# Channel attention, then a GELU feed-forward in split precision: Strassen's seven products in the second layer too, in chunks of 512 tokens

## The chip, the cores and the metric

The kernel runs on 1 core of a Trainium2 chip. The metric is device time in microseconds; before the change it is 2187.15 us (median of three runs, 2186.88 to 2187.25). TensorE does the matmuls, VectorE (DVE) and ScalarE (ACT) the elementwise work, GpSimd (POOL) next to nothing, SyncE (SP) issues the transfers. SBUF is the on-chip memory of 128 partitions, PSUM the accumulators of the matmuls: 8 banks, each 128 partitions by 512 fp32 values.

## The reference

```python
# attention: B, N, C = 4, 6080, 256
qn = q / (norm(q, axis=1, keepdims=True) + 1e-06)        # k likewise
s = kn.transpose(0, 2, 1) @ qn / tau                     # 256 x 256 for each of 4 batches
a = softmax(s, axis=-1)
x = (v @ a).reshape(24320, 256)
# feed-forward: w_in 256 x 2048, w_out 2048 x 256
h = x @ w_in
g = 0.5 * h * (1.0 + erf(h / sqrt(2)))
out = g @ w_out
```

The weights reach the kernel as fp64 words and are narrowed on the chip.

## The kernel before, in words

**Numbers.** Each fp32 operand is split into a high part in fp32r, the matmul format, and a low part with the rest. A product is three matmuls: low weight by high data, high by high, high weight by low data. Making a pair costs an ACT write of the high part and a DVE subtraction for the low part.

**Stages.** For each batch, the scores of q and k give `a`; `w_group` (L365) folds `a` into `w_in`, so that the feed-forward's first layer takes v directly. Batch 0's scores come first, alone. Those of batch b+1 are made in small pieces during the feed-forward of batch b: `extras` (L653) puts pieces behind each step: `load_qk`, `split_qk` (L178), `burst` (L186, which adds its PSUM bank to `sacc` at L201), `norm_part` (L203), the softmax, and the next `w_group`s.

**Feed-forward.** A batch's 6080 tokens are cut into 6 pairs of token blocks (five of 2 x 512 tokens, one of 2 x 480), and the 2048 hidden features into 8 units u of 256. One step is (batch, pair, unit).

- First layer (`first_products`, L484): the step's block of h, 2 feature rows by 2 token columns, by Strassen's seven products in Winograd's form, with the v forms (B11, T1, ...) and weight forms (A11, S1, ...) prepared ahead by `v_sums`, `v_split` and `w_sums`. Seven products of three 512-column matmuls (L458 to L460). Three partial sums are copied to SBUF by ACT (`kept`, L491), three joins are DVE additions of a PSUM bank and such a copy (`added`, L496). Then `gelu` (L462) twice on ACT, to high format (L466) and to fp32 (L467), and a DVE subtraction for the low part (L468).
- Second layer (`second_products`, L528): the plain way, 2 token blocks x 2 feature rows x 2 output halves, three matmuls each (L541 to L543), 24 matmuls a step, summed over the eight units in four PSUM banks `po`. After the last unit ACT and DVE move them to `osb`, and they go out.
- The first pair of batch 0 uses plain products in both layers (`plain_products`, L471), while `narrow_unit` (L576) still narrows weights.

**Order.** The program is written so that each yield of the first layer's product is followed by one part of the *previous* step's second layer (L714, L715): on TensorE, first-layer and second-layer matmuls alternate in threes. From this order a planner makes each engine's queue: it may take a later instruction ahead where an earlier one would not be ready by its own costs. Each queue then runs strictly in its order on the chip. `issue_after` (in `behind`, L105) holds named instructions behind a mark.

**Buffers.** PSUM: four banks `ph` for the first layer, bursts and weight groups (`bank`, L111), four for `po`. `w_out` units come back from a DRAM copy (`keep_out`, L255) through three `wo` buffers, one load of 512 KB a step (`load_wo`, L268).

## Time and profile before

| | |
|---|---|
| time of the runs | 2187.15 us (2186.88 to 2187.25) |
| profiled execution, its span | 2185.0 us (the page gives no other time of that execution) |
| TensorE matmuls, weight loads | 9664, 9664 |
| TensorE / DVE / ACT busy | 2174.5 / 1392.8 / 1437.0 us |
| matmul groups of the two layers, L458-460 and L541-543 | 1564.0 us and 1800.0 us, with overlap |
| DMA | 267.52 MB, mean 122 GB/s |

The page sums an instruction from its start to its modelled end. Neighbours on one engine overlap, so the spacing of starts in a timeline, not the mean of one instruction, is what a long queue costs. Where a line has several shapes, the answers that keep shapes apart are used.

### The profile page before, as it was taken

How to read it: one execution, taken by the hardware profiler on the slowest of the kernel's cores; microseconds unless marked ns; L12 is line 12 of the kernel's file. 1: busy time of each engine (PE TensorE's matmuls, PEld its weight loads, DVE VectorE, ACT ScalarE, POOL GpSimd, SP SyncE). 2: the span in 40 equal slices, each digit the busy share in tenths (PEclk: the TensorE clock that was granted, in tenths of full speed). 3: DMA queues.
4: the chain of work that ended last, by engine and by line, in shares of the span. 5: the costliest groups of instructions: out<-in, count | busy, mean ns of one | idle time of the engine just before them, and what ended most of it. 6: DMA issues, size and time to landing. Idle time of an engine off the chain costs nothing.

```text
span 2185.0 us, 26209 instructions
## 1 busy us (share of the span) xinstructions
PE 2174.5 (100%) x9664; PEld 1793.9 (82%) x9664; DVE 1392.8 (64%) x2179; ACT 1437.0 (66%) x2595; POOL 1.3 (0%) x8
## 2 busy tenths in 40 slices
PE   9999999999999999999999999999999999999999
PEld 7788888888888888888888888888888888888888
DVE  6995767656676575675667757657466555555554
ACT  6666666667666666676765666667576566666665
POOL 0000000000000000000000000000000000000000
PEclk9999999999999999999999999999999999999999
DMA  9562534422343353542323335343132122121121
GB/s 380 189 211 106 174 133 157 160 90 87 106 144 105 118 173 116 174 154 67 105 92 134 122 116 174 133 153 128 49 112 97 58 89 71 65 97 66 68 78 47
DMA packets 77056, 267.52 MB, mean 122 GB/s; under 512 B 7680, under 2 KB 9728, under 8 KB 74880
## 3 DMA queue, kind: packets, MB, share of 16 engines
q1 hardware_dynamic: 76928, 265.84, 35.2%
q8 instruction: 76, 1.25, 0.2%
q14 instruction: 52, 0.43, 0.1%
HBM read 232.52 MB, written 33.29 MB: 122 GB/s over the span
## 4 chain that ended last, share of the span: by engine, by line
PE 97%; DVE 2%; DMA 1%; issue 0%; ACT 0%; SPq 0%; DVEq 0%; ACTq 0%
PE po L543 16%; PE po L541 16%; PE po L542 16%; PE ph L460 14%; PE ph L459 14%; PE ph L458 14%; PE ph L191 3%; PE ph L193 1%; DMA raw<-qk 1%; DVE acc L139 1%; PE ph L378 1%; PE ph L376 1%; PE ph L377 1%; PE ph L149 0%; DVE nt L247 0%
## 5 line engine op out<-in xcount | busy, mean ns | idle before, releaser
L468 DVE TENSOR_TENSOR gl<-g,gh 128x512 fp32r<-128x512 f32 (+1 forms) x768 | 521.7, 682 | 145.3 <-ACT g L467 142.7
L543 PE MATMUL po<-gl,wo 128*128 128x512 f32 (+1 forms) x1536 | 605.2, 394 | 0.0
L541 PE MATMUL po<-gh,wo 128*128 128x512 f32 (+1 forms) x1536 | 599.2, 390 | 0.6 <-ACT gh L466 0.6
L542 PE MATMUL po<-gh,wo 128*128 128x512 f32 (+1 forms) x1536 | 595.6, 388 | 0.0
L496 DVE TENSOR_TENSOR h<-ph,p 128x512 f32<-128x512 f32 (+1 forms) x368 | 252.0, 685 | 531.4 <-PE ph L460 452.6
L460 PE MATMUL ph<-vl,wh 128*128 128x512 f32 (+1 forms) x1336 | 522.7, 391 | 0.0
L459 PE MATMUL ph<-vh,wh 128*128 128x512 f32 (+1 forms) x1336 | 521.5, 390 | 0.0
L458 PE MATMUL ph<-vh,wl 128*128 128x512 f32 (+1 forms) x1336 | 519.8, 389 | 0.7 <-DVE wl L363 0.7
L466 ACT ACTIVATE gh<-h 128x512 fp32r<-128x512 f32 (+1 forms) x552 | 345.2, 625 | 236.8 <-DVE h L496 232.8
L491 ACT COPY p<-ph 128x512 f32<-128x512 f32 (+1 forms) x368 | 213.4, 583 | 241.4 <-PE ph L460 240.3
L542 PEld LDWEIGHTS po<-gh,wo 128*128 128x128 f32 x1536 | 288.4, 188 | 64.0
L541 PEld LDWEIGHTS po<-gh,wo 128*128 128x128 f32 x1536 | 288.4, 188 | 62.3 <-ACT gh L466 1.0
L543 PEld LDWEIGHTS po<-gl,wo 128*128 128x128 f32 x1536 | 288.4, 188 | 61.5
L467 ACT ACTIVATE g<-h 128x512 f32<-128x512 f32 (+1 forms) x552 | 337.5, 611 | 0.0
L459 PEld LDWEIGHTS ph<-vh,wh 128*128 128x128 f32 x1336 | 251.1, 188 | 56.9
L458 PEld LDWEIGHTS ph<-vh,wl 128*128 128x128 f32 x1336 | 251.0, 188 | 53.2 <-DVE h L496 1.4
L460 PEld LDWEIGHTS ph<-vl,wh 128*128 128x128 f32 x1336 | 250.9, 188 | 51.0
L491 ACT COPY u<-ph 128x512 f32<-128x512 f32 (+1 forms) x184 | 106.9, 581 | 106.6 <-PE ph L460 106.6
L466 ACT ACTIVATE gh<-ph 128x512 fp32r<-128x512 f32 (+1 forms) x216 | 125.3, 580 | 22.9 <-PE ph L460 18.2
L467 ACT ACTIVATE g<-ph 128x512 f32<-128x512 f32 (+1 forms) x216 | 126.5, 586 | 1.6 <-DVE gl L468 1.5
L496 DVE TENSOR_TENSOR h<-ph,u 128x512 f32<-128x512 f32 (+1 forms) x184 | 125.4, 682 | 2.8
L209 ACT ACTIVATE kqc<-kqc 128x1024 f32<-128x1024 f32 x72 | 76.4, 1061 | 36.1 <-DMA kqc<-kqt 36.0
(135 smaller groups left out, 1354.0 us busy)
## 6 DMA issues: line engine op xcount, KB each, us to landing
wo<-keep_out SPq DMA_DIRECT2D x184, 512.0 KB, 3.3
raw<-qk SPq DMA_DIRECT2D x95, 512.0 KB, 4.3
kqc<-kqt SPq DMA_DIRECT2D x72, 512.0 KB, 4.4
v_raw<-vt SPq DMA_DIRECT2D x20, 1024.0 KB, 5.5
out<-osb SPq DMA_DIRECT2D x40, 512.0 KB, 3.3
win<-keep_in SPq DMA_DIRECT2D x12, 1024.0 KB, 4.8
keep_in<-win SPq DMA_DIRECT2D x4, 1024.0 KB, 4.6
keep_out<-wo SPq DMA_DIRECT2D x8, 512.0 KB, 3.6
```

The costliest lines, as they stand in the source:

```text
L209: nc.scalar.activation(out=x, in_=x, func=AF.Square, accum_out=state["nsum"][:, t, c:c + 1])
L458: nc.tensor.matmul(ps[:, :n], wl, hi[:, :n], start=start, stop=False, skip_group_check=True)
L459: nc.tensor.matmul(ps[:, :n], wh, hi[:, :n], start=False, stop=False, skip_group_check=True)
L460: marks["product"] = nc.tensor.matmul(ps[:, :n], wh, lo[:, :n], start=False, stop=stop, skip_group_check=True)
L466: nc.scalar.activation(out=gh[:, :n], in_=src, func=AF.Gelu)
L467: marks["gelu"] = nc.scalar.activation(out=g[:, :n], in_=src, func=AF.Gelu)
L468: nc.vector.tensor_tensor(out=gl[:, :n], in0=g[:, :n], in1=f32(gh[:, :n]), op=ALU.subtract)
L491: nc.scalar.copy(out=t[:, :n], in_=ps[:, :n])
L496: nc.vector.tensor_tensor(out=h[:, :n], in0=ps[:, :n], in1=t[:, :n], op=ALU.add)
L541: nc.tensor.matmul(o, wo[:, 1, i, cs], gh[:, :n], start=first, stop=False)
L542: nc.tensor.matmul(o, wo[:, 0, i, cs], gh[:, :n], start=False, stop=False)
L543: nc.tensor.matmul(o, wo[:, 0, i, cs], gl[:, :n], start=False, stop=last)
```

## The change

**Chunks.** After the first pair the unit of work is a chunk of 512 tokens (480 at a batch's end), cut in two halves of 256 (240), by a group g of 512 features: 46 chunks x 4 groups. `chunk_products` does the first layer's seven products with two output rows q each, so 42 matmuls of 256 columns. The v forms of a chunk have double buffers.

**First layer's joins.** ACT copies product 1 into another PSUM bank `px`, and product 4 accumulates on it; DVE writes product 3's sum plus product 2's copy into a bank `pz`, and product 6 accumulates on that. Copies go from 3 to 2, additions from 3 to 2.

**Second layer.** `sums` makes four combinations (T1 to T4) of the GELU blocks, splits them, and `chunk_out` takes seven products of 2 x 3 matmuls of 256 columns with weight forms A and S (`CROSS`), summed over the groups in four banks and joined at the chunk's end on ACT and DVE. The block B12 then needs only its fp32 GELU. The last chunk of batches 0 to 2 (`plain_out`) keeps plain second-layer products of 480 columns.

**Weights of the second layer.** `wo_sums` makes the S forms once, with 24 additions on POOL, in the first pair; eight forms are kept in DRAM, and seven (1.79 MB) are loaded for each step, in four loads with a buffer each (`load_part`), each issued when the same part of the step before has been used (`load_next`).

**Other.** PSUM: two banks `ph`, one `px`, one `pz`; bursts and weight groups of later batches take turns with the products in the two `ph` banks. The high copies of `split_qk` and of `w_sums` are on ACT. `kqc` and `osb` have one buffer. The written order still alternates, now in sixes; the join of product 7 and `sums` come after the last of the previous step's second-layer products, and the extras after them.

```diff
+CHUNKS = [(t + j * n, n // 2) for t, n in PAIRS for j in range(2)]
+NCH = len(CHUNKS)
+H = NT // 2
...
+FORMS = ("S4", "A11", "A12", "S3", "S1", "S2", "A21", "A22")
+CROSS = (("S4", "B22"), ("A11", "B11"), ("A12", "B21"), ("S3", "T3"), ("S1", "T1"), ("S2", "T2"), ("A22", "T4"))
+SLOT = {"T2": 0, "T4": 1, "T1": 2, "T3": 3, "B12": 3, "B11": 4, "B22": 5, "B21": 6}
+GSLOT = {"B11": 0, "B12": 1, "B22": 2, "B21": 3}
+BLOCK = {(1, 0): "B22", (0, 1): "B11", (1, 1): "B21", (0, 0): "B12"}
...
-    ps_h = ctx.enter_context(tc.tile_pool(name="ps_h", bufs=4, space=bass.MemoryType.PSUM))
+    ps_h = ctx.enter_context(tc.tile_pool(name="ps_h", bufs=2, space=bass.MemoryType.PSUM))
+    ps_x = ctx.enter_context(tc.tile_pool(name="ps_x", bufs=1, space=bass.MemoryType.PSUM))
...
+        state["bank"] = at = (state.get("bank", -1) + 1) % 4
+        if at % 2 and "halves" not in state:
+            return ps_x.tile([P, NT], F32, name="px" if at == 1 else "pz")
         return ps_h.tile([P, NT], F32, name="ph")
...
-        nc.vector.tensor_copy(out=hl[:, 0], in_=raw)
+        nc.scalar.copy(out=hl[:, 0], in_=raw)
...
+    def load_part(b, c, g, i):
+        at, to = parts(b, c)[i]
+        t = pw.tile([P, 2, 2, 2, P], F32R, name="wo", bufs=4)
+        marks["wo"] = nc.sync.dma_start(out=f32(t[:, 0:to - at]), in_=keep_out[g][:, at:to])
+        for f in range(at, to):
+            wos[b, c, g, FORMS[f]] = t[:, f - at]
...
+    def wo_sums(g):
+
+        first = pqk.tile([P, 2, 4, 2, P], F32, name="hl")
+        fa, fs = first[:, 0], first[:, 1]
+        hl = pqk.tile([P, 4, 2, 2, P], F32R, name="hl")
+        tt = nc.gpsimd.tensor_tensor
+        for q in range(2):
+            wo = wos[0, 0, 2 * g + q]
...
+            tt(out=fa[:, :, q], in0=v[0], in1=v[1], op=ALU.add)
...
+        tt(out=s4, in0=a12, in1=s2, op=ALU.subtract)
+        nc.scalar.copy(out=hl[:, :, 0], in_=fs)
+        nc.vector.tensor_tensor(out=hl[:, :, 1], in0=fs, in1=f32(hl[:, :, 0]), op=ALU.subtract)
...
+        copy = nc.scalar.copy
...
+    def v_sums(b, c):
+        x, h = v_half(b, c)
         tt = nc.vector.tensor_tensor
-        if half == 0:
-            ts = vts[b, p] = [pv.tile([P, NT], F32, name=f"vs{i}") for i in range(4)]
-            tt(out=ts[0][:, :n], in0=x[0, 1], in1=x[0, 0], op=ALU.subtract)
-            tt(out=ts[2][:, :n], in0=x[1, 1], in1=x[0, 1], op=ALU.subtract)
+        t = vts[b, c] = pv.tile([P, 4, H], F32, name="vs")
+        tt(out=t[:, 0:2, :h], in0=x[:, :, 1], in1=x[:, 0], op=ALU.subtract)
+        tt(out=t[:, 2, :h], in0=x[:, 1, 1], in1=t[:, 0, :h], op=ALU.subtract)
+        tt(out=t[:, 3, :h], in0=x[:, 1, 0], in1=t[:, 2, :h], op=ALU.subtract)
...
         def do(i, ps, start, stop):
-            product(b, p, u, *ORDER[i], ps, start, stop)
-
-        one = bank()
+            a, v = ORDER[i]
+            at = VSLOT[v]
+            for q in range(2):
+                o = ps[:, q]
+                nc.tensor.matmul(o, wls[g][:, a, q], vh[:, at, :h], start=start and q == 0, stop=False,
+                                 skip_group_check=True)
+                nc.tensor.matmul(o, whs[g][:, a, q], vh[:, at, :h], start=False, stop=False,
+                                 skip_group_check=True)
+                marks["product"] = nc.tensor.matmul(o, whs[g][:, a, q], vl[:, at, :h], start=False, stop=stop,
+                                                    skip_group_check=True)
...
+        def block(at, src):
+            name = BLOCK[at]
+            whole = halves(gs[:, GSLOT[name]], h)
+            nc.scalar.activation(out=whole, in_=src, func=AF.Gelu)
+            if name == "B12" and not plain:
+                return
+            hi, lo = (halves(t[:, SLOT[name]], h) for t in (his, los))
+            nc.scalar.activation(out=hi, in_=src, func=AF.Gelu)
+            tt(out=lo, in0=whole, in1=f32(hi), op=ALU.subtract)
+
+        def sums():
+            t, hi, lo = (x.rearrange("p i (q n) -> p i q n", q=2)[:, :, :, :h] for x in (gs, his, los))
+            tt(out=t[:, 0:2], in0=t[:, 1:3], in1=t[:, 0:2], op=ALU.subtract)
+            nc.scalar.copy(out=hi[:, 2:4], in_=t[:, 0:2])
+            tt(out=t[:, 2], in0=t[:, 2], in1=t[:, 0], op=ALU.subtract)
+            tt(out=t[:, 3], in0=t[:, 3], in1=t[:, 2], op=ALU.subtract)
+            nc.scalar.copy(out=hi[:, 0:2], in_=t[:, 2:4])
+            tt(out=lo[:, 2:4], in0=t[:, 0:2], in1=f32(hi[:, 2:4]), op=ALU.subtract)
+            tt(out=lo[:, 0:2], in0=t[:, 2:4], in1=f32(hi[:, 0:2]), op=ALU.subtract)
+
+        one = halves(ps_h.tile([P, NT], F32, name="ph"), h)
         do(0, one, True, False)
-        p1 = kept(one, "p1")
-        yield
-        two = bank()
-        do(1, two, True, False)
-        p5 = kept(two, "p5")
+        x = halves(ps_x.tile([P, NT], F32, name="px"), h)
+        nc.scalar.copy(out=x, in_=one)
+        yield
+        two = halves(ps_h.tile([P, NT], F32, name="ph"), h)
+        do(1, two, True, True)
+        p5 = halves(pg.tile([P, NT], F32, name="p5", bufs=2), h)
+        nc.scalar.copy(out=p5, in_=two)
         yield
         do(2, one, False, False)
-        u2 = kept(one, "u2")
-        yield
-        three = bank()
-        do(3, three, True, True)
-        out[1, 0] = gelu(added(three, p1), n)
+        z = halves(ps_x.tile([P, NT], F32, name="pz"), h)
+        tt(out=z, in0=one, in1=p5, op=ALU.add)
+        yield
+        do(3, x, False, True)
+        block((1, 0), x)
         yield
         do(4, one, False, False)
-        out[0, 1] = gelu(added(one, p5), n)
-        yield
-        do(5, two, False, True)
-        out[1, 1] = gelu(added(two, u2), n)
+        tt(out=p5, in0=one, in1=p5, op=ALU.add)
+        block((0, 1), p5)
+        yield
+        do(5, z, False, True)
+        block((1, 1), z)
         yield
         do(6, one, False, True)
-        out[0, 0] = gelu(one[:, :n], n)
+        yield
+        block((0, 0), one)
+        if not plain:
+            sums()
 
...
+        for i, (form, v) in enumerate(CROSS):
+            if first and i % 2 == 0:
+                po["banks"].append(new_bank())
+            o = po["banks"][i // 2][:, i % 2]
+            w = wos.pop(key + (form,))
+            for q in range(2):
+                mh, ml = (halves(m[:, SLOT[v]], h)[:, q] for m in (his, los))
+                nc.tensor.matmul(o, w[:, 1, q], mh, start=first and i % 2 == 0 and q == 0, stop=False,
+                                 skip_group_check=True)
+                nc.tensor.matmul(o, w[:, 0, q], mh, start=False, stop=False, skip_group_check=True)
+                nc.tensor.matmul(o, w[:, 0, q], ml, start=False, stop=last and q == 1, skip_group_check=True)
+            if i % 2 or i == 6:
+                load_next(key, i // 2)
+            if last:
+                banks = po["banks"]
+                if i == 0:
+                    osb = new_osb()
+                    pq = state["pq"] = pg.tile([P, 4, H], F32, name="pq", bufs=1)[:, :, :h]
+                elif i == 1:
+                    nc.scalar.copy(out=pq[:, 0:2], in_=banks[0])
+                elif i == 3:
+                    tt(out=osb[:, 1], in0=banks[1][:, 0], in1=pq[:, 1], op=ALU.add)
+                    nc.scalar.copy(out=pq[:, 3], in_=banks[1][:, 1])
+                elif i == 5:
+                    nc.scalar.copy(out=pq[:, 2], in_=banks[2][:, 0])
+                    tt(out=osb[:, 2], in0=banks[2][:, 1], in1=pq[:, 1], op=ALU.add)
+                    tt(out=osb[:, 0:4:3], in0=pq[:, 2:4], in1=osb[:, 2:3].broadcast_to([P, 2, h]), op=ALU.add)
+                    tt(out=osb[:, 0], in0=osb[:, 0], in1=pq[:, 0], op=ALU.add)
+                    tt(out=osb[:, 2], in0=osb[:, 3], in1=pq[:, 2], op=ALU.add)
+                elif i == 6:
+                    tt(out=osb[:, 3], in0=banks[3][:, 0], in1=osb[:, 3], op=ALU.add)
+                    done()
+            yield
...
+    def extras(b, w):
+
+        c, g = divmod(w, NWG)
...
+            nxt = (b, c + 1) if c + 1 < NCH else (b + 1, 0)
+            if nxt[0] < B:
+                if c % 2 and g == 0:
+                    load_v(nxt[0], nxt[1] // 2)
+                if g == 1:
+                    v_sums(*nxt)
+                elif g == 2:
+                    v_split(*nxt, 0)
+                elif g == 3:
+                    v_split(*nxt, 1)
+                    v_split(*nxt, 2)
...
+    state["halves"] = True
+    many = 2
+    for b in range(B):
+        for c in range(0 if b else 2, NCH):
+            for g in range(NWG):
+                for _ in chunk_products(b, c, g):
+                    for _ in range(many):
+                        next(second, None)
+                for _ in second:
+                    pass
+                extras(b, c * NWG + g)
+                second = chunk_out(b, c, g)
+                many = 2 if plain_out(b, c) else 1
```

What is left out of the diff: renamed arguments, the first pair's products (as before), the plain second layer of a batch's last chunk, and the load order.

317 lines of the change are left out of this document (190 added, 127 removed).

## The prediction

> **What bounds the kernel now.** I read the page's shares first, then the chain of work that ended last, then what TensorE waited for.
>
> ```profile
> span 2185.0 us, 26209 instructions
> PE 2174.5 (100%) x9664; PEld 1793.9 (82%) x9664; DVE 1392.8 (64%) x2179; ACT 1437.0 (66%) x2595; POOL 1.3 (0%) x8
> PEclk9999999999999999999999999999999999999999
> PE 97%; DVE 2%; DMA 1%; issue 0%; ACT 0%; SPq 0%; DVEq 0%; ACTq 0%
> ```
> ```profile
> PE ph L149 <- DMA raw<-qk: 4.7, 3, 3.7
> PE po L319 <- DVE diag L314: 0.8, 1, 0.8
> PE ph L458 <- DVE wl L363: 0.7, 1, 0.7
> PE po L541 <- ACT gh L466: 0.6, 1, 0.6
> ```
>
> TensorE sets the end at full clock. Its waits are 6.8 us in all, while DVE and ACT have a third of the span free. So the change can gain only by TensorE time, and can lose by taking that free third. The time is therefore read from the spacing of matmul starts. Three pairs of batch 3 (each window runs from a pair's first product to the next pair's), a stretch of a burst with all engines, and two rows of a 480-column stretch:
>
> ```profile
> 1766.30:1849.20 82.90, 82.90 (x362) 67.64 (x361) 44.99 (x70) 54.10 (x98) 0.00 (x0) 1.00 0.22 77
> sum 248.60, PE 248.60 PEld 202.85 DVE 134.62 ACT 162.09 POOL 0.00; mean PE 82.87 PEld 67.62 DVE 44.87 ACT 54.03 POOL 0.00
> ```
> ```profile
> 1010.97 0.40 PE L191 MATMUL ph<-hl 128*128 128x512 f32 x1
> ...
> 1011.21 0.28 PE L193 MATMUL ph<-hl 128*128 128x256 f32 x1
> 1011.21 0.19 PEld L191 LDWEIGHTS ph<-hl 128*128 128x128 f32 x1
> ...
> 1011.32 0.39 PE L191 MATMUL ph<-hl 128*128 128x512 f32 x1
> ...
> 1011.55 0.28 PE L193 MATMUL ph<-hl 128*128 128x256 f32 x1
> ...
> 1012.25 0.28 PE L193 MATMUL ph<-hl 128*128 128x256 f32 x1
> ...
> 1012.56 0.69 DVE L201 TENSOR_TENSOR sacc<-ph,sacc 128x512 f32<-128x512 f32 x1 [0.58 <-PE ph L193]
> ...
> 1013.29 0.42 DVE L290 TENSOR_TENSOR t<-sacc 128x256 f32<-128x256 f32 x1
> ...
> 1013.75 0.39 PE L458 MATMUL ph<-vh,wl 128*128 128x512 f32 x1
> ...
> 1013.95 0.69 DVE L201 TENSOR_TENSOR sacc<-ph,sacc 128x512 f32<-128x512 f32 x1 [0.23 <-PE ph L193]
> ```
> ```profile
> 2172.01 0.38 PE L460 MATMUL ph<-vl,wh 128*128 128x480 f32 x1
> ...
> 2172.66 0.38 PE L543 MATMUL po<-gl,wo 128*128 128x480 f32 x1
> ```
>
> A pair is 8 x 45 = 360 matmuls: 82.87 / 360 = 0.230 us per 512 columns. Eight neighbours L191 + L193 take 1013.75 - 1010.97 = 2.78 us; less 0.230 for the 512, a 256-column matmul costs 0.117 us. Of 480 columns, three take 0.65 us: 0.217 each. A consumer starts 0.03 us after its matmul (1012.25 + 0.28 to 1012.56). And the planner does take later instructions ahead: L290, written behind both burst additions L201, runs between them.
>
> **Matmuls.** Removed: 23 pairs x 360. Added: 43 chunks x 4 x 84 = 14,448 of 256 (240) columns, and for the three plain chunks 504 of 240 and 288 of 480. A 512 pair becomes 672 x 0.117 = 78.6 us, 4.25 less; nineteen give -81. A 240-column matmul still has a full weight load beside it; I price it at 0.117 too, so the 480 pairs (360 x 0.217 = 78.1) become 78.6 in batch 3 and 504 x 0.117 + 96 x 0.217 = 79.8 in the others: +6. Sum **-75 us**. Bounds: 14,952 small matmuls make 15 us of each ns. At half of the 512's cost (0.115) it is -105; 0.120, the larger spacing that rounding of these rows allows, gives -30.
>
> The Trainium skill, "TensorE: Matmul & The Clock Gate", Part 3, says that a weight load overlaps running matmuls only where the row groups differ. By that each small matmul would wait for its load. The trace disagrees: the load for L191 and the 256-column L193 both start at 1011.21, and L191 follows 0.11 us later.
>
> **DVE and ACT.** Prices, from the answer that keeps shapes apart and a DVE timeline:
>
> ```profile
> L491 ACT COPY p<-ph 128x512 f32<-128x512 f32 x304 | 177.9, 587 | 219.3 <-PE ph L460 218.7
> L467 ACT ACTIVATE g<-ph 128x512 f32<-128x512 f32 x184 | 108.6, 591 | 1.6 <-DVE gl L468 1.5
> L182 DVE TENSOR_TENSOR hl<-raw,hl 128x1024 fp32r<-128x1024 f32 x68 | 82.4, 1218 | 0.7
> L396 DVE TENSOR_TENSOR hl<-hl 128x256 f32<-128x256 f32 x16 | 6.8, 422 | 9.5 <-ACT hl L379 9.5
> L403 ACT CAST wh<-hl 128x1024 fp32r<-128x1024 f32 x4 | 4.3, 1076 | 0.4 <-DVE hl L399 0.4
> ```
> ```profile
> 222.30 0.69 DVE L201 TENSOR_TENSOR sacc<-ph,sacc 128x512 f32<-128x512 f32 x1
> 222.90 1.22 DVE L182 TENSOR_TENSOR hl<-raw,hl 128x1024 fp32r<-128x1024 f32 x1
> 224.04 0.69 DVE L181 CAST hl<-raw 128x1024 fp32r<-128x1024 f32 x1
> ```
>
> In a queue a 512-wide DVE operation costs 0.60 us and a 1024-wide one 1.14. A cross step has seven of the first (two joins, three low parts, two sums) and three of the second (one sum, two low parts): 7.6 us, and 0.2 more where a sum needs the one just before. A chunk's v forms and output joins are five of 512 and eight of 256 (0.42): 6.4 us, 1.6 a step. DVE: **9.4 us a step**, against 84 x 0.117 = **9.83 on TensorE**. In batches 0 to 2 the scores and weight groups of the next batch add 1.2 to DVE (per batch 24 low parts at 1.14, 24 additions at 0.60, 4 x 3.8 of weight sums, over 48 steps) and 0.93 to TensorE (12 x 2.78 and 48 x 0.23): 10.6 against 10.76. DVE goes from 64% to about 97% of TensorE. ACT, at full durations: two copies, five GELUs from PSUM, two of B11 (priced alike), two 1024 copies, 7.5 us, and about 0.9 per step for v forms and joins. The moved `split_qk` and weight copies fit there.
>
> No row shows ACT or DVE writing PSUM, as x and z do. The nearest are those that read it: 587 and 690 ns. I take these; 0.1 us more or less stays under the slack of x (C0, P1, C1 lie between) and z (C2, P3, C3).
>
> **Waits that it adds.** Call the groups of six matmuls, 0.70 us each, P0 to P6 (first layer) and C0 to C6 (second layer of the step before). The restart after a wait is dearer than the wait:
>
> ```profile
> 253.67 0.40 PE L543 MATMUL po<-gl,wo 128*128 128x512 f32 x1
> ...
> 253.85 0.68 DVE L496 TENSOR_TENSOR h<-ph,u 128x512 f32<-128x512 f32 x1
> ...
> 253.99 0.50 PE L458 MATMUL ph<-vh,wl 128*128 128x512 f32 x1
> ...
> 254.33 0.40 PE L459 MATMUL ph<-vh,wh 128*128 128x512 f32 x1
> ```
>
> The second matmul comes 0.34 after the first instead of 0.23: 0.11 us on top.
>
> - *Step's end.* With two `ph` banks, P0 takes the bank that P6 filled, so it waits for B12's GELU: 0.28 - 0.117 + 0.03 + 0.59 + 0.05 = 0.83 us after P6's slot, and C6 covers 0.70. In the written order 0.13 + 0.11 = 0.24 x 172 cross steps = 41 us; 0 where the planner puts C0 there. I take 14, as L290 shows that it fills such places, though by its own costs.
> - *Bursts.* They take the same two banks, so the next P0 waits for DVE's addition, which may stand behind sums. 34 pairs of bursts (the 272 instances of L193 by eight): nothing if the second burst's 1.39 us covers it, about 1.5 us each (51) if not. Taken: 14.
> - *First pair.* DVE is full there:
>
> ```profile
> 60.00:110.00 50.00, 48.77 (x211) 39.03 (x210) 49.85 (x97) 35.89 (x65) 0.00 (x0) 1.00 0.49 168
> 110.00:160.00 50.00, 50.00 (x219) 40.73 (x218) 47.98 (x85) 32.45 (x59) 0.00 (x0) 1.00 0.59 202
> ```
>
> POOL's 24 additions (8 of 512, 16 of 256) have no row; at DVE's 0.60 and 0.42 they are 11.5 us. Between nothing and twice that I take 6, since four 1.14 us low parts come to DVE for certain. The Trainium skill, "SBUF — State Buffer", on the two sides of SBUF, says that POOL and a DVE operation with two SBUF inputs take turns on a shared port, one blocking the other fully. By that rule the whole 11.5 us or more would fall on DVE; POOL is idle here, so no row tells.
> - *Tail.* The last C3 waits for sums with no P beside it: +3.
> - *Rest:* late DVE or ACT here and there, 0 upward, the upper end being the second rival; taken: 6.
>
> **Sum:** -75 + 14 + 14 + 6 + 3 + 6 = -32. The span 2185.0 becomes 2153; the runs' median lies 2.15 above the span, so **2155 us**, 1.5% faster. Its own range is 2115 to 2185.
>
> **Rivals.**
>
> 1. *Nothing waits, and a small matmul is exactly half.* -105 + 9: 2091. For it: TensorE's 6.8 us of waits now. Against: DVE's slack falls to a few per cent.
> 2. *Slower: ACT's queue.* `sums` runs DVE, ACT, DVE. From P6's end: B12's GELU until 0.78, first sum 2.03, two more 3.47, the second high copy until 4.58. If x's copy stands behind it, it ends at 5.17 and P2 starts at 5.22, where TensorE was ready at 0.94 + 4 x 0.70 = 3.74: 1.48 + 0.11 = 1.6 us. In all 172 steps +275; in every second, with the -75 and +9: 2258. It decides from one step in four, 66 / 1.6 = 41 steps. For it: DVE 97% loaded, queues strictly in order. Against: x is ready before the second high copy, and the planner sees readiness.
> 3. *The small matmul is dearer in an unbroken stream.* At 82.87 / 672 = 0.1233 the gain is gone; at 0.123, with the waits, 2245. That is the change not doing what it says: 16,624 matmuls for a fifteenth fewer columns. The burst rows speak against it, but there every second matmul has 512 columns.
> 4. *Loads of weight forms come late.*
>
> ```profile
> DMA packets 77056, 267.52 MB, mean 122 GB/s; under 512 B 7680, under 2 KB 9728, under 8 KB 74880
> ...
> wo<-keep_out SPq DMA_DIRECT2D x184, 512.0 KB, 3.3
> ```
>
> A step needs 1.84 MB in 9.83 us, 187 GB/s, where one 512 KB load in 10.4 us was 51; the mean of all traffic goes from 122 GB/s to some 260. Each part is issued 12 groups, 8.4 us, ahead and lands in some 3.3 now. Behind an issue that waits for its buffer on SP stand the loads of q, k and v. One us in the 124 cross steps of batches 0 to 2 would give 2279.
> 5. Every small matmul waits for its load (the first rule above): with 0.19 us for each of 14,952 loads, 2155 + 2841, about 5000.
>
> **Chances.** Forecast 0.42, rival 1 0.13, rival 2 0.28, rival 3 0.08, rival 4 0.04, rival 5 0.01, gain and waits cancelling 0.04. Within 0.2% (4.4 us) counts as no change. Faster: 0.41 + 0.13 = 0.54; same 0.06; slower 0.40. The range 2080 to 2270 leaves out a quarter of rival 1, some 0.12 of rival 2, half of rival 4 and rival 5: about 0.19.
>
> **What would show it.** Small matmuls' starts 0.117 apart; TensorE's waits for B12's GELU or for a copy x below 0.3 us a step; DVE above 90%; wo loads landing within 8 us. It is wrong if TensorE waits more than 0.4 us a step (then the gain is gone), above all before P2 for x's copy, or if the spacing reaches 0.123.

## The result, and the profile after

The changed kernel takes **2383.02 us** (median of four runs, 2381.37 to 2385.87) against 2187.2: a ratio of 1.0898, 95% interval 1.0883 to 1.0914. It is 196 us slower, where 32 less were forecast. Its page, and what TensorE waited for (the columns after the colon are us in total, times, longest):

```profile
span 2381.6 us, 42310 instructions
PE 2225.0 (93%) x16624; PEld 2110.3 (89%) x16624; DVE 1984.6 (83%) x2879; ACT 1640.7 (69%) x2788; POOL 48.5 (2%) x32
```
```profile
PE ph L555 <- ACT px L585: 41.9, 21, 4.1
PE po L713 <- ACT his L578: 13.3, 15, 1.7
PE po L716 <- DVE los L580: 12.2, 20, 0.8
PE ph L555 <- DVE pz L594: 9.3, 13, 1.3
PE po L716 <- DVE los L579: 9.1, 13, 1.6
```

TensorE is no longer full, and the longest wait in total is that of P2 (L555) for x's copy (L585), 41.9 us in 21 places. No engine is over 93% of the span, which points to lateness rather than to an engine at its limit; the experiments test it. The mean granted clock fell from 1.00 to 0.982.

Where the 195 us lie, by the starts of each stretch's first product in the trace (us; a batch's 12 chunks as ten of 512 tokens, in batch 0 eight, and the last two of 480). Beside the two kernels stand three of the experiments below: 1, 3 and the last kernel of 9 ("all mendings", whose last two chunks have 512 and 448 tokens):

| stretch | before | after | x's copy first | matmuls alone | all mendings |
|---|---|---|---|---|---|
| up to the first chunk | 157.2 | 174.8 | 175.1 | 173.9 | 162.9 |
| batch 0, eight chunks | 360.1 | 385.4 | 384.5 | 356.5 | 360.8 |
| batch 0, last two | 87.2 | 114.6 | 107.7 | 89.0 | 106.6 |
| batch 1, ten chunks | 450.9 | 473.7 | 462.7 | 437.4 | 443.3 |
| batch 1, last two | 87.3 | 117.0 | 108.3 | 89.0 | 100.5 |
| batch 2, ten chunks | 450.9 | 475.1 | 460.4 | 438.5 | 445.4 |
| batch 2, last two | 87.3 | 115.5 | 106.1 | 89.7 | 103.1 |
| batch 3, ten chunks | 416.9 | 412.1 | 412.4 | 401.8 | 411.6 |
| batch 3, last two | 83.3 | 107.9 | 90.9 | 80.3 | 88.0 |
| last matmul at | 2181.1 | 2376.0 | 2308.1 | 2156.2 | 2222.3 |

More than half of the loss, 110 us, lies in the last two chunks of the four batches; 72 in the ten-chunk stretches of batches 0 to 2, which carry the next batch's scores; 18 ahead of the first chunk. Only the ten chunks of batch 3 are faster, by 4.8. The view of stretches for these and the two chunks behind them (columns: window, its length, busy time and count of PE, PEld, DVE, ACT, POOL; granted clock, DMA share, GB/s):

```profile
1856.10:2268.20 412.10, 412.06 (x3344) 404.70 (x3343) 366.19 (x522) 295.00 (x506) 0.00 (x0) 1.00 0.60 199
2268.20:2376.00 107.80, 90.86 (x714) 88.59 (x714) 74.38 (x102) 58.57 (x103) 0.00 (x0) 0.92 0.46 153
```

In the first the view shows no idle time of TensorE. In the second it is idle for 17 us and runs at a mean clock of 0.92. One such place, on ACT and then on TensorE (start, duration; in brackets the idle time and what ended it):

```profile
2291.68 0.58 ACT L565 ACTIVATE gs<-ph 128x480 f32<-128x480 f32 x1
2293.59 1.00 ACT L575 CAST his<-gs 128x960 fp32r<-128x960 f32 x1 [1.33 <-DVE gs L574]
2295.03 0.99 ACT L578 CAST his<-gs 128x960 fp32r<-128x960 f32 x1 [0.44 <-PE po L716]
2295.93 0.55 ACT L585 COPY px<-ph 128x480 f32<-128x480 f32 x1
```
```profile
2292.67 0.27 PE L559 MATMUL ph<-vlo,wh 128*128 128x240 f32 x1
...
2294.68 0.27 PE L716 MATMUL po<-los,wo 128*128 128x240 f32 x1
2296.53 0.38 PE L555 MATMUL ph<-vhi,wl 128*128 128x240 f32 x1 [1.58 <-ACT px L585]
```

P0 ends at 2292.94, so its bank could be copied then, and ACT was idle. But in ACT's queue B12's GELU, both high copies of the sums (L575, L578) and only then x's copy follow each other. It ends at 2296.48, where 2293.5 was possible, and P2 waits 1.58. This is the prediction's second rival. In 15 of the 23 steps of 240 columns that follow such sums the copy stands behind both, in the other 8 between them; of the 148 such steps of 256 columns it stands ahead of both in 109.

### The profile page after: what moved, and what is told of

It is laid out like the page before. It is cut to its first block, busy times and chain, and to the rows that moved or that the text cites. A ratio compares the mean times of both kernels' runs of the same rounds, so it can differ in the third digit from the quotient of the medians.

```text
span 2381.6 us, 42310 instructions
## 1 busy us (share of the span) xinstructions
PE 2225.0 (93%) x16624; PEld 2110.3 (89%) x16624; DVE 1984.6 (83%) x2879; ACT 1640.7 (69%) x2788; POOL 48.5 (2%) x32
## 4 chain that ended last, share of the span: by engine, by line
PE 50%; ACT 15%; DMA 15%; DVE 14%; issue 4%; POOL 1%; SPq 1%; POOLq 0%; ACTq 0%; DVEq 0%
DMA kqc<-kqt 12%; PE po L716 8%; PE po L713 7%; PE po L715 7%; PE ph L555 6%; PE ph L559 5%; PE ph L557 5%; ACT gs L565 4%; ACT his L569 4%; ACT kqc L222 2%; ACT his L578 2%; DVE gs L574 2%; DMA v_raw<-vt 2%; DVE los L580 2%; PE px L555 1%
## 5 line engine op out<-in xcount | busy, mean ns | idle before, releaser
L713 PE MATMUL po<-his,wo 128*128 128x256 f32 (+1 forms) x2408 | 691.6, 289 | 21.2 <-ACT his L578 13.3
L716 PE MATMUL po<-los,wo 128*128 128x256 f32 (+1 forms) x2408 | 677.9, 290 | 21.6 <-DVE los L580 12.2
L715 PE MATMUL po<-his,wo 128*128 128x256 f32 (+1 forms) x2408 | 681.0, 284 | 0.0
L555 PE MATMUL ph<-vhi,wl 128*128 128x256 f32 (+1 forms) x1840 | 533.4, 291 | 79.2 <-ACT px L585 41.9
L570 DVE TENSOR_TENSOR los<-gs,his 128x512 fp32r<-128x512 f32 (+1 forms) x564 | 381.1, 684 | 215.4 <-ACT his L569 211.8
L557 PE MATMUL ph<-vhi,wh 128*128 128x256 f32 (+1 forms) x1840 | 515.1, 280 | 0.0
L559 PE MATMUL ph<-vlo,wh 128*128 128x256 f32 (+1 forms) x1840 | 513.9, 280 | 0.0
L713 PEld LDWEIGHTS po<-his,wo 128*128 128x128 f32 x2408 | 463.1, 192 | 35.0 <-ACT his L578 21.0
L716 PEld LDWEIGHTS po<-los,wo 128*128 128x128 f32 x2408 | 453.4, 192 | 37.4 <-DVE los L580 17.2
L715 PEld LDWEIGHTS po<-his,wo 128*128 128x128 f32 x2408 | 462.4, 192 | 0.2
L555 PEld LDWEIGHTS ph<-vhi,wl 128*128 128x128 f32 x1840 | 350.5, 191 | 104.6 <-ACT px L585 47.2
L580 DVE TENSOR_TENSOR los<-gs,his 128x1024 fp32r<-128x1024 f32 (+1 forms) x172 | 208.9, 1215 | 54.9 <-ACT his L578 54.4
L578 ACT CAST his<-gs 128x1024 fp32r<-128x1024 f32 (+1 forms) x172 | 178.8, 1040 | 90.0 <-DVE gs L577 88.6
L575 ACT CAST his<-gs 128x1024 fp32r<-128x1024 f32 (+1 forms) x172 | 180.3, 1048 | 52.3 <-DVE gs L574 52.2
L579 DVE TENSOR_TENSOR los<-gs,his 128x1024 fp32r<-128x1024 f32 (+1 forms) x172 | 208.6, 1213 | 7.3 <-ACT his L575 7.0
```

Of the source, the lines that this page charges most:

```text
L555: nc.tensor.matmul(o, wls[g][:, a, q], vh[:, at, :h], start=start and q == 0, stop=False, skip_group_check=True)
L557: nc.tensor.matmul(o, whs[g][:, a, q], vh[:, at, :h], start=False, stop=False, skip_group_check=True)
L559: marks["product"] = nc.tensor.matmul(o, whs[g][:, a, q], vl[:, at, :h], start=False, stop=stop, skip_group_check=True)
L570: tt(out=lo, in0=whole, in1=f32(hi), op=ALU.subtract)
L578: nc.scalar.copy(out=hi[:, 0:2], in_=t[:, 2:4])
L579: tt(out=lo[:, 2:4], in0=t[:, 0:2], in1=f32(hi[:, 2:4]), op=ALU.subtract)
```

## The experiments

Times are medians of four runs, or of one run where the kernel leaves work out (3, 7, and two kernels of 9); the kernel before, run beside them, took 2185.8 to 2186.7. Line numbers move by a few where an edit adds lines.

**1. x's copy ahead of the sums' copies**

```diff
-        nc.scalar.copy(out=x, in_=one)
+        marks["x"] = nc.scalar.copy(out=x, in_=one)
+        with behind("x"):
+            state.pop("late", lambda: None)()
...
-            sums()
+            state["late"] = sums
```

> Undone: the place of x's copy in ACT's queue. The sums of a step are written after the next step's copy of P0 into the x bank, and both high copies of the sums stand behind that copy on ACT, so P2 never waits for them; everything else is as in the changed kernel. Theory A (rival 2 of the prediction, ACT's order): the trace of the changed kernel counts about 80 us of P0-to-P2 excess (57 in the 240-column chunks, 24 in the others) and some 43 us lost to half clock, about half of it behind these waits; expected 2383 - 80 - 20, about 2280, with TensorE's waits on x's copy under 10 us in sum. Theory B (ACT and DVE are late whatever the order, since sums begin only after B12): the sums come later by the copy's 0.6 us, TensorE's wait moves from P2 to the second layer's groups that use sums; expected 2350 to 2390.

Measured: 2317.78 us, ratio 1.0600 (1.0584 to 1.0616), 65 less than the changed kernel. TensorE's wait for this copy has shrunk, and the clock is 0.990:

```profile
PE ph L555 <- ACT px L585: 5.1, 7, 1.4
```

Of the 68 us in the table 42 are in the last two chunks and 26 in the ten-chunk stretches of batches 1 and 2. Theory A's mechanism holds, for a third of the loss; its 2280 was too low, and 131 us remain.

**2. The last 960 tokens as 512 + 448**

```diff
-CHUNKS = [(t + j * n, n // 2) for t, n in PAIRS for j in range(2)]
+CHUNKS = [(t, min(NT, N - t) // 2) for t in range(0, N, NT)]
...
-        at = c % 2 * 2 * h
+        at = CHUNKS[c][0] - PAIRS[c // 2][0]
```

> One size changed: the last 960 tokens of a batch are cut as 512 + 448 (halves of 256 and 224 columns) in place of 480 + 480 (halves of 240). In the changed kernel these last two chunks cost 116.3 us in batch 1 and 107.9 in batch 3, 26 and 25 more than the same stretch of the kernel before, while ten 512-token chunks cost 412 in batch 3, two less than before. Theory A (the planner puts x's copy behind both high copies in the 240-column steps, in most 256-column ones not): chunk 10 becomes like the chunks before it, chunk 11 keeps at most a few late copies; about 20 us less in each of four batches, about 2305. Theory F (a short chunk is dear because the fixed parts of the ACT and DVE instructions do not shrink with the columns): chunk 10 is healed, chunk 11 gets worse than one 240-column chunk; some 8 us less per batch, about 2350.

Measured: 2320.27, ratio 1.0610 (1.0586 to 1.0635), 63 less. Chunk 10 falls from 48.3 to 41.1 us in batch 3 and from 54.6 to 43.9 in batch 1; chunk 11 falls as well, from 59.6 to 51.6. In the 23 steps named above x's copy now stands ahead of both high copies in 15. So this mends the same late copy by another way, as experiment 5 confirms; theory F falls.

**3. Matmuls alone**

```diff
-        do(0, one, True, False)
-        x = halves(ps_x.tile([P, NT], F32, name="px"), h)
-        nc.scalar.copy(out=x, in_=one)
+        do(0, one, True, True)
+        x = halves(ps_x.tile([P, NT], F32, name="px"), h)
```

and so for p5, z, the GELUs and the sums.

> Left out: in every chunk step the copies of P0 and P1, the additions in z and p5, the GELUs, the sums and their splits; each accumulation of the first layer starts itself, and the second layer reads what the first pair left in the split tiles. All matmuls, loads, splits of v, output additions and the next batch's scores stay. Theory C (the stream of small matmuls itself costs what the gain was to be): in batch 3 a 512-token chunk took 41.25 us for 336 matmuls, 0.1228 each, with hardly a wait; if this stays (about 41 us a chunk), 14,952 x (0.1228 - 0.117) = 87 of the forecast's 75 us gain are gone before anything waits, and the whole comes to about 2215, slower than before without one wait of the first layer. Rival (the restarts of some 0.1 us between groups come from instructions that stop at a semaphore of ACT or DVE): without these the spacing is 0.118, a chunk 39.7, the whole about 2145.

Measured: 2164.1 in one run, 22 less than before. The stretch of batch 3:

```profile
1674.10:2075.90 401.80, 401.55 (x3342) 400.64 (x3341) 66.97 (x129) 37.28 (x71) 0.00 (x0) 1.00 0.65 205
2075.90:2156.20 80.30, 80.30 (x716) 80.13 (x715) 6.40 (x14) 3.94 (x10) 0.00 (x0) 1.00 0.66 206
```

The first window holds 3318 matmuls of 256 columns and 24 of 480, as its first step carries the plain second layer of batch 2's last chunk. By their starts one of 256 columns takes **0.1196 us** here, with nothing to wait for, and 0.1226 in the changed kernel; the 671 of 240 columns behind them take 0.112. The difference is some hundred spacings of 0.2 us or more (100 in the changed kernel, 1 here): a tenth of a us too much each, 10 in all. 84 of the 100 are ahead of second-layer matmuls, but for only 35 does the trace show a semaphore to wait for. So they come with ACT's and DVE's work; how they arise stays open. Both theories are half right. And with nothing of ACT's and DVE's chunk work to wait for, this change gains 22 us, or, by an estimate, 30 to 40 with the next experiment's mending.

**4. The sums of the output weights on DVE**

```diff
-        tt = nc.gpsimd.tensor_tensor
+        tt = nc.vector.tensor_tensor
```

> One engine changed: the 24 additions that form the sums of the output weights in the first pair run on DVE in place of POOL. In the changed kernel POOL's take 4 to 9 us each where they are 512 wide, and the first chunk starts at 174.8 us where the kernel before started its second pair at 157.2: 17.6 us more, where 6 was forecast. Theory E (the slow POOL additions delay the tiles and hold DVE's or PE's work up): on DVE they take about 0.6 and 0.4 us, 11.5 in all, and the first chunk starts at 163 to 168; 7 to 12 us less in all. Rival (DVE is full there, so what counts is work and not the engine): it starts at 175 to 185; 0 to 10 us more.

Measured: 2365.88, ratio 1.0823 (1.0798 to 1.0848), 17 less; the first chunk starts at 163.9, and its first step takes 10.7 us where it took 19.7. The groups of the 512-wide additions, of the changed kernel and of this one (busy, mean ns of one):

```profile
L304 POOL TENSOR_TENSOR hl<-wo 128x512 f32<-128x512 f32 x8 | 32.7, 4091 | 128.8 <-DVE wl L451 76.4 <-DVE wo L265 21.4 <-DMA keep_out<-hl 18.9
```
```profile
L304 DVE TENSOR_TENSOR hl<-wo 128x512 f32<-128x512 f32 x8 | 5.4, 684 | 0.0
```

An addition took 4.1 us in the mean on POOL (four of them 1.3 to 1.7, four 4.6 to 9.3) and 0.68 on DVE, though DVE was busy for 104 of the last 107 us ahead of the first chunk. The Trainium skill, "SBUF — State Buffer", on the two separate sides, has POOL and a DVE operation with two SBUF inputs lock each other out. POOL's uneven times would fit that, but no run shows POOL beside an idle DVE, nor that DVE lost by it.

**5. The mendings of 1, 2 and 4 together, and then a later second layer.** The second kernel starts the second layer's groups only behind P2:

```diff
-                for _ in chunk_products(b, c, g):
-                    for _ in range(many):
+                for i, _ in enumerate(chunk_products(b, c, g)):
+                    for _ in range(many if many == 2 or i > 1 else 0):
```

> The three mendings together: the last 960 tokens as 512 + 448, x's copy ahead of the sums' copies on ACT, the additions of the output weights' sums on DVE. If each heals its own loss: 2383 - 65 (x's copy) - 17 (DVE) = 2301, and the 448 cut, whose own -63 lay in the same late copies, adds between 0 and -10: 2290 to 2301. If the losses replace each other: 2305 or more.

> As the three mendings together, and one order changed: the second layer's groups are written two first-layer groups later (C0 behind P2 in place of P0; the last two behind P6), so that the sums have 1.4 us more before the group that needs them, and two groups cover the step's end. Theory L (what is left is the latency of the chain GELU, sums, high copies, low parts): TensorE's waits on the sums' results (30 us in the kernel with x's copy moved) and at the step's end go, 30 to 45 us less than without the shift, about 2255. Theory W (DVE has too much work where the next batch's is added): the waits move to other places; within 10 us of the kernel without the shift. The other side: the groups' banks and weight tiles are held longer, the weights come later; 10 or more us slower.

Measured: 2299.21, ratio 1.0514 (1.0493 to 1.0535), and 2304.28, 1.0537 (1.0519 to 1.0554). 2318 less experiment 4's 17 is 2301, so the 448 cut adds next to nothing beside x's copy. 1.4 us more for the sums do not help, so theory L falls.

**6. One part alone: a plain second layer everywhere**

```diff
-        return c == NCH - 1 and b < B - 1
+        return True
```

> One part of the change alone: the first layer per 512-token chunk in halves of 256, its joins on copies in PSUM, and the second layer plain in all chunks (24 matmuls of 512 columns a step, as the changed kernel has it in the last chunk of batches 0 to 2). No sums, no high copies of sums. Theory C (small matmuls at the 0.1196 of the kernel without ACT and DVE work): the first layer costs 42 x 0.1196 - 21 x 0.230 = 0.19 us a step more than before, 184 steps, 36 us, and the first pair 12 to 17: 2235 to 2240, with hardly a wait. Rival (copies and joins in PSUM make TensorE wait by themselves): above 2260. The other side (256 columns cost half of 512, 0.115): 2195 to 2205.

Measured: 2449.64, ratio 1.1202 (1.1186 to 1.1219), 210 above the expectation. Ten chunks of batch 3 take 465.6 us; 42 x 0.1196 + 24 x 0.230 = 10.54 us a step would be 422. The answer on waits names the cause:

```profile
PE po L689 <- ACT his L569: 102.6, 145, 1.5
```

The plain second layer waits 0.7 us, 145 times in 132 of the 184 steps, for a high copy of a GELU block that ACT has only just made; 30 of the 44 us in this stretch are such waits. So the time is the rival's (above 2260), but the cause is not the copies and joins in PSUM that it named. The expectation had priced TensorE's work only. In this order the seven products of the second layer are faster, 412 against 466; but no run took the waits out of the plain order, and without them, by the estimate of 422, the products would be worth about 10.

**7. Without the next batch's work, and its pieces**

```diff
-        if n0 <= w < n0 + 2 * NCT * NSC:
+        if False:
```

and so for bursts, splits, loads and softmax. The further kernels leave out one piece each.

> The kernel with x's copy ahead of the sums' copies, and left out: the next batch's scores (bursts on TensorE, their loads, the ACT copy and the DVE subtraction of each split, the DVE additions), its norms and its softmax; the weights of batches 1 to 3 are formed from batch 0's attention. This removes about 36 us of matmuls from batch 1 and as much from batch 2 (the stretch of ten chunks: 437.4 there against 401.8 in batch 3 where nothing but matmuls was left). Theory B (what is still lost in batches 0 to 2 is ACT and DVE being late with this extra work on them): batch 1 falls from 571 us to that of batch 3, 503, plus a few for the weights, about 510; the whole about 2140. Rival (the loss is in the chunk steps themselves): batch 1 falls by the 36 us of matmuls alone, to 535; the whole about 2215.

> The kernel with x's copy ahead of the sums' copies, and left out: all but the first of each batch's splits of the next batch's q and k (ACT's copy of about 1.05 us and DVE's subtraction of about 1.2 us, 20 to 24 a batch); the bursts on TensorE all read the first split. Loads, bursts and their additions stay. Without any of the next batch's work, ten chunks of batch 1 fell from 462.7 to 411.7 us, of which 36 are matmuls; 15 us a batch are due to the rest. Theory W (the engines' work as such): the splits are about half of what ACT and DVE have to do for it, so 6 to 10 us a batch, 2290 to 2300. Theory K (the bursts take the two banks that P0 and P1 need, and hold them until DVE has added): nothing, 2312 to 2320.

> The kernel with x's copy ahead of the sums' copies, and left out: DVE's additions of the bursts' banks, all but the last of each batch (0.69 us each, two a burst step). A burst's bank is then free as soon as TensorE has filled it. Theory K (the banks): the 15 us a batch go, about 2275, and the waits of P0 and P1 on these additions with them. Theory W (work as such): a third of the extra DVE work, 3 to 5 us a batch, about 2305.

Measured: 2169.93 without all of it; ten chunks take 411.7 us in batches 1, 2 and 3, with no wait over 0.25 us. So what x's copy left in these stretches comes from the next batch's work: 462.7 - 411.7 - 36 of matmuls = 15 us. The last two chunks do not gain by it: 105 to 107 us in batches 0 to 2, where experiment 1 has 106 to 108. But 2316.18 without the splits and 2322.09 without the additions (462.7 becomes 459.8 and 463.9): neither is it.

**8. Orders and the last chunk**

```diff
-                for t in range(NB):
-                    split_qk(b + 1, k * NB + t)
+                later.append(lambda k=k: [split_qk(b + 1, k * NB + t) for t in range(NB)])
```

> The kernel with x's copy ahead of the sums' copies, and one order changed: the splits of the next batch's q and k and the squares of its norms are written behind the sums of the step, in place of ahead of them. Nothing is left out. Theory O (what costs is that such a piece, 1.05 to 1.2 us, stands in ACT's or DVE's queue between two links of the sums' chain): TensorE's waits on the sums' results (about 13 us in batch 1) halve, 5 to 10 us a batch, about 2295. Theory W (total work): 2310 to 2325.

> The kernel with x's copy ahead of the sums' copies, and the last chunk of batches 0 to 2 computed by seven products in the second layer too, as the last chunk of batch 3. That chunk took 57.5 to 59 us with the plain second layer, 7 to 9 more than the 50.2 of the kernel that had matmuls alone, and the last chunk of batch 3, without the next batch's weights (48 matmuls of 512 columns, 11 us), 48.0. Theory Q (the plain second layer waits for the late low parts of its own blocks: all chunks plain gave 46.5 us a chunk where matmuls alone make 42.2): 2 to 6 us less per batch, about 2305. Rival (the next batch's weights keep ACT and DVE full, and sums come on top): 48 + 11 and more, 59 to 65; 2318 to 2335.

Measured: 2342.93, ratio 1.0723 (1.0705 to 1.0741), and 2377.87, 1.0880 (1.0864 to 1.0896): 25 and 60 more than experiment 1. Both theories of late_extras fall. Without the plain second layer the last chunk takes 65 to 67 us instead of 57.5 to 59; and the ten-chunk stretches behind grow too, by 11 in batch 1, 18 in batch 2 and 7 in batch 3. Of that 9, 11 and 8 lie in the stretch's first chunk, whose first step carries the second layer of the chunk before. The rest, up to 7 us, is in chunks that the edit does not touch; experiment 2 moved the ten chunks of batch 2, which it does not touch, by 7 as well, and there the planner's queues have another order. So a few us in one stretch can come from that alone.

**9. The load of the norms.** What batch 1's ten chunks lose in experiment 1 against matmuls alone lies in chunks 2 to 8, mostly; the norms' pieces are written in chunks 2 to 7. ACT's wait for their loads, in the kernel before and in the changed one:

```profile
ACT kqc L209 <- DMA kqc<-kqt: 36.0, 42, 1.9
```
```profile
ACT kqc L222 <- DMA kqc<-kqt: 81.7, 60, 3.5
```

One of them in the kernel of experiment 1: the load's issue on SP (its last numbers are the first and the last start), then ACT, DVE and TensorE by the timeline:

```profile
L221 SPq DMA_DIRECT2D kqc<-kqt x1: 425/425/425, 1003.5 to 1003.5; - x1
```
```profile
1009.54 1.06 ACT L222 ACTIVATE kqc<-kqc 128x1024 f32<-128x1024 f32 x1 [1.88 <-DMA kqc<-kqt]
1010.50 0.19 ACT L222 ACTIVATION_READ_ACCUMULATOR kqc<-kqc 128x1 f32 x1
1010.59 1.03 ACT L578 CAST his<-gs 128x1024 fp32r<-128x1024 f32 x1
```
```profile
1011.65 1.23 DVE L580 TENSOR_TENSOR los<-gs,his 128x1024 fp32r<-128x1024 f32 x1 [1.29 <-ACT his L578]
```
```profile
1011.67 0.39 PE L715 MATMUL po<-his,wo 128*128 128x256 f32 x1 [1.81 <-ACT his L578]
```

The load, issued at 1003.5, has landed six us later. ACT stands 1.88 us for it with the sums' high copy behind, and TensorE waits 1.81 for that copy. On SP this load stands behind the weight forms' loads, and those wait for their buffers (the changed kernel's row; the kernel before has 1413.6 us of such waits, so they are not new):

```profile
SPq L291 <- PE po L716: 1406.9, 629, 9.2
```

The change also cuts this tile's buffers from two to one, but the trace does not bear that out as the cause: in the changed kernel each load is issued more than 2.2 us after the square before it has ended, 5.6 in the median, and with two buffers it was 4.9. In both kernels ACT comes to the square at once, 5.5 and 4.7 us after the issue, and the load takes that long to land. What grew is the landing, by a us (median; before, then changed); why it grew no run shows:

```profile
kqc<-kqt SPq DMA_DIRECT2D x72, 512.0 KB, 4.4
kqc<-kqt SPq DMA_DIRECT2D x72, 512.0 KB, 5.4
```

A first try wrote the square one step after its load (`state["square"] = square`, called by the next step's extras); two more put this on top of experiment 5, the second with DVE's sums of v a step later.

> The kernel with x's copy ahead of the sums' copies, and one order changed: the square of a piece of the next batch's norms is written one step after its load in place of right behind it; tile, buffer and work are the same. In the changed kernel this tile has one buffer where it had two, and ACT waits 82 us in 60 places for its load where it waited 36 in 42. The waits of TensorE in batch 1 begin in the step of the first such piece and end with the last. Theory N (ACT stands at the head of its queue for this load, and the copies and GELUs behind it come late): ACT's wait for it goes to nothing, ten chunks of batch 1 fall from 462.7 us to about 448 (411.7 without the next batch's work, and 36 of matmuls), 40 to 50 us in all with batches 0 and 2: 2270 to 2280. Rival (the amount of work): 2310 to 2320.

> All mendings together: the last 960 tokens as 512 + 448, x's copy ahead of the sums' copies, the sums of the output weights on DVE, and the square of a norms' piece one step after its load. If the losses are separate: 2299 (the first three) less 40 to 50, 2250 to 2260. If the planner's new order brings others: 2270 or more. In no case below the kernel before, 2187, as the matmuls alone took 2164.

> As all_mended, and DVE's sums of the next chunk's v written one step later, with the first split, so that the load of v has two steps in place of one. In the kernel with x's copy moved DVE stood 12 us in 13 places for it, and in one place of batch 1 the join z came 2.8 us late behind it and TensorE fell to half clock. Theory V: 10 to 20 us less than all_mended. Rival (the sums of v, packed with the splits into fewer steps, press on DVE there): the same or up to 15 more.

Measured: 2304.97, ratio 1.0547 (1.0531 to 1.0563); 2282.54, 1.0443 (1.0427 to 1.0459); 2276.40, 1.0417 (1.0398 to 1.0435). In none did the wait go (69, 78 and 78 us): the planner put the square early in the step again (in the first of these kernels a load issued at 755.9 has its square at 761.6, and such a load lands in 5.5). Of the gains of the first two, 13 and 17 us, 6 and 12 lie in batch 0's eight chunks; the stretches of batches 1 and 2 fall by 1 to 4, which is within what experiment 8 puts down to another order. So the loads were taken away, and then every piece but the bursts' matmuls, their loads, the softmax and the weights. The first of the two edits:

```diff
+                state["kqc"] = pg.tile([P, NS], F32, name="kqc", bufs=1)
+                nc.gpsimd.memset(state["kqc"], 1.0)
```

> The kernel with x's copy ahead of the sums' copies, and left out: the loads of the norms' pieces for batches 1 to 3 (72 of 512 KB). The squares stay, on a tile that is filled once, so ACT has the same work and never waits for such a load (79 us in 61 places). Theory N (ACT stands at the head of its queue for the load): ten chunks of batch 1 fall from 462.7 us to about 448; with the other two batches 40 to 45 us less, 2270 to 2280. Rival (the squares as work, 1.06 us each; or the bursts themselves): 455 to 463 in batch 1, 2300 to 2318.

> The kernel with x's copy ahead of the sums' copies, and left out of the next batch's work: the splits but the first, the additions of the bursts' banks but the last, the loads and squares of the norms. The bursts' matmuls, their loads of q and k, the softmax and the weights stay. Theory A/D (ACT's and DVE's work or waits for the next batch, in whatever share): ten chunks of batch 1 take the 411.7 us without the next batch and 36 of matmuls, 448; about 2270. Rival (the bursts themselves: four groups of matmuls that TensorE puts between a step's groups and that take the two banks of P0 and P1): 455 to 463, about 2305.

Measured: 2285.99 and 2262.65. Ten chunks of batch 1 fall from 462.7 to 442.5 without the loads alone, of batch 2 from 460.4 to 443.3, and the eight of batch 0 from 384.5 to 369.3: 52 us, theory N's 40 to 45 and more. Without the other pieces they are 439.9, 439.2 and 368.7, so those cost next to nothing beside the loads. In the first kernel a wait of 8.8 us for a join in batch 0 came up, and the last two chunks there took 23 more; its cause was not sought. Last, the square tied to where the load has landed, on top of all_mended_v:

```diff
-            nc.scalar.activation(out=hi, in_=src, func=AF.Gelu)
+            marks[name] = nc.scalar.activation(out=hi, in_=src, func=AF.Gelu)
...
+        with behind(*(["B21"] if "B21" in marks else [])):
+            state.pop("square", lambda: None)()
```

> As all_mended_v, and the square of a norms' piece tied behind the GELU of the third block of the step after its load, so that ACT comes to it some 9 us after the load's issue, where the load lands in 5.6. Nothing is left out. Theory N: ACT's wait for these loads (78 us) goes nearly to nothing and the ten-chunk stretches of batches 0 to 2 fall by 10 to 20 us each: 2225 to 2250. Rival (the square in its new place, 1.06 us ahead of the next x copy, costs what the wait did): 2265 to 2280. In no case below the kernel before.

Measured: **2230.59**, ratio 1.0201 (1.0184 to 1.0218), 46 less than all_mended_v. ACT waits for no such load any more, though the tile still has one buffer. The fall lies in the three stretches that have norms' pieces, 11, 18 and 18 us; the ten chunks of batch 3, which have none, stay at 411.6. The page, and the stretch of batch 1:

```profile
span 2228.6 us, 42408 instructions
PE 2173.0 (98%) x16624; PEld 2091.1 (94%) x16624; DVE 1975.4 (89%) x2903; ACT 1635.9 (73%) x2788; POOL 1.3 (0%) x8
```
```profile
635.00:1079.00 444.00, 441.05 (x3552) 432.26 (x3551) 412.67 (x586) 346.51 (x586) 0.00 (x0) 1.00 0.74 243
```

The ten-chunk stretches of batches 1 to 3 are now 5 to 8 us faster each than before the change. No version beats the kernel before. Of the 44.6 us that are left, 53 lie in the last two chunks of the batches and 6 ahead of the first chunk, and the ten-chunk stretches give 18 back; some 3 come behind the last matmul. In batch 1's last chunk there TensorE waits 2.5 us for the weight groups' bank, 2.3 for one join z and little else, at 57.0 us where matmuls alone took 50.2. Over the last two chunks of all four batches TensorE's waits sum to 26 us, and windows of half clock take at most 9. Why ACT and DVE are late there was not settled.

## Why the prediction was wrong

**What bounds the kernel** was read rightly: gain only by TensorE's time, loss by the free third of DVE and ACT.

**Matmuls, -75.** The price of 0.117 came from bursts of eight. In the long stream it is 0.1196 for 256 columns and 0.112 for 240: 12,768 x 0.0026 - 2,184 x 0.005 = +22, so -53, inside the bounds given. The small stops raise it to 0.1226 in batch 3; if they are as many everywhere, they take another 38 of the gain (12,768 x 0.0030), which leaves about -15. The third rival had 0.123 as the place where the gain is gone; that is nearly what was met, though by single stops and not by every matmul. The fifth rival, a wait for every weight load, did not come.

**DVE and ACT: the step that failed.** DVE at 9.4 us a step against TensorE's 9.83 was right enough: 366 us busy of 412 in batch 3, 89%, without a wait of TensorE. What failed is what was made of it. The prediction summed work, let an engine with room never be late, and put lateness into the term "rest" at 6 us. The runs show instead that TensorE's waits from the first chunk on are 130 us, 0.7 a step, where 0.4 had been named as the sign of being wrong. ACT was 69% busy, and yet the two largest losses that an experiment undid, 65 and 46 us, came from its queue, because an instruction that waits there, for a sum or a load, holds everything behind it.

**The second rival** was the right mechanism: x's copy behind the second high copy, 1.6 us in the place shown. "The planner sees readiness" was the argument against it, and it failed: in 15 of the 23 steps of 240 columns the planner placed the copy behind both. Its price left something out: such a wait can be followed by 3.4 us or more of half clock, as 6 of 14 gaps of 2.0 to 2.4 us were (last section). Undone, it gives back 65 us.

**Loads.** The fourth rival looked at the right queue and asked only whether wo comes late. It does not: its loads land in 4.2 us. It named the loads of q, k and v that stand behind on SP, but not the norms' piece. ACT waited 36 us for that load even before, hidden under its free third; this row was in the trace of before and not quoted. It cost about 50 us (52 by the stretches without the loads, 46 by the square moved), the largest item without any term in the sum.

**First pair, +6** was +18, and 9 more in the first step: POOL's additions were priced at DVE's 0.60 and took 4.1. On DVE they leave the first chunk 7 us later than before the change.

**Step's end and bursts (+28)** were the wrong places: the bursts' additions cost nothing (experiment 7), and no wait at the step's end is among the large ones.

**Clock.** Nothing in the prediction had the granted clock move.

**What stays open.** The mendings give back 152 of the 196 us. The last two chunks of the four batches still take 53 us more than before the change; 26 of them are seen as waits of TensorE, and no run settles what makes them.

## What to carry to other kernels

Where an engine's queue is strictly in order, ask of each new instruction on the critical chain what may stand ahead of it and what that one waits for; a busy share of 69% says nothing on it. A change that lives off an engine's free time also lives off the time that hid its waits. So list that engine's waits for loads in the trace of before, also those that cost nothing there, and ask how long after its issue each load is used. And before the waits are argued, the most that a change can gain is worth a run of its matmuls alone: here 22 us, against the 75 that the sum began with.

## What the runs showed of the hardware

**Half clock after short waits.** In the changed kernel 19 windows of 3.4 or 6.8 us, 82 us together, have half the clock ahead of the last matmul, which is at most 41 us of work lost; the kernel before has none there. An instance in the kernel of experiment 1, where DVE stood 0.78 us for the load of v ahead of the join z, and then the stretches behind it:

```profile
1138.63 0.69 DVE L488 TENSOR_TENSOR vs<-v_raw 128x512 f32<-128x512 f32 x1 [0.78 <-DMA v_raw<-vt]
1139.24 0.66 DVE L596 TENSOR_TENSOR pz<-ph,p 128x480 f32<-128x480 f32 x1
...
1139.95 0.57 PE L555 MATMUL ph<-vhi,wl 128*128 128x240 f32 x1 [2.77 <-DVE pz L596]
1140.32 0.41 PE L557 MATMUL ph<-vhi,wh 128*128 128x240 f32 x1
```
```profile
1139.90:1143.30 3.40, 3.35 (x15) 3.35 (x16) 2.30 (x5) 1.44 (x4) 0.00 (x0) 0.50 0.14 58
1143.30:1146.50 3.20, 3.20 (x18) 3.20 (x18) 1.87 (x4) 1.52 (x4) 0.00 (x0) 0.56 0.05 8
1146.50:1149.00 2.50, 2.50 (x24) 2.50 (x24) 2.47 (x5) 1.19 (x3) 0.00 (x0) 1.00 0.75 232
```

By these clocks the wait of 2.77 us costs some 3 us more in the 6.6 behind it. The Trainium skill, "TensorE: Matmul & The Clock Gate", Part 1, has the clock drop after an idle window of about 3.4 us that runs free of the kernel, and return after a busy one. The lengths of the windows agree. But here shorter gaps were enough: in the changed kernel such a window followed 6 of 14 gaps of 2.0 to 2.4 us between matmul starts, and 10 of 14 longer ones. It followed three gaps of about 1 us too, but each of these had another of 1.2 to 1.9 us beside it.

**Below 240 columns a matmul got no cheaper.** In the free stream 256 columns cost 0.1196 us and 240 cost 0.112, in proportion. Of 224 columns there is no free stream; in the last kernel those that do not stop start 0.112 apart, where 0.105 would be in proportion.
